# Linear attention on one core: transposes in two halves, and one store in three pieces

## The chip, the cores and the metric

The kernel runs on 1 core of one Trainium2 chip. The metric is the device time in microseconds. A run of the kernel is compared with runs of the kernel before on the same chip. The profile is of one execution; its span goes from the first to the last instruction, and the measured time has about one microsecond around it.

## The reference

```python
# q, k, v: (1, 32, 2048, 128) bf16
phi_q = jnp.where(q > 0, q + 1, jnp.exp(q)) + 1e-6
phi_k = jnp.where(k > 0, k + 1, jnp.exp(k)) + 1e-6
kv = jnp.einsum("bhsd,bhse->bhde", phi_k, v)
z = jnp.einsum("bhsd->bhd", phi_k)
num = jnp.einsum("bhqd,bhde->bhqe", phi_q, kv)
den = jnp.einsum("bhqd,bhd->bhq", phi_q, z)[..., None] + 1e-6
return num / den
```

There are 32 heads, and each is independent of the others: a 128 x 128 matrix kv with the sum z beside it is built from k and v, and each row of q is multiplied by it and divided by its denominator.

## The kernel before

One head is 2048 rows of 128 numbers. A row block lies as 128 partitions with 16 consecutive rows each, so that a load or a store of a head is one transfer of 512 KB in which each partition holds 4 KB in one piece, in SBUF and in DRAM alike. The 16 rows of a partition are the 16 "tiles" j of the head. Loads have 7 buffers for each of q, k and v (`NI`), the output has 12 (`NO`).

The function phi is computed as min(exp(x), 1) + 1e-6 plus max(x, 0). The two parts are never added; both go through TensorE and are summed in PSUM. For each head h there are these steps, named as in the order lists:

- **ldk, ldq, ldv** (L338): the loads, issued by SP in a list written out by hand; ldv0 alone is issued by ScalarE.
- **ek** (L350, ScalarE) is exp(k); **em** (L353, VectorE) the minimum and the 1e-6 on it; **rkp** (L360, GpSimd) max(k, 0), for head 0 half of it as **rkd** (L356, VectorE); **v1** (L364, GpSimd) copies v beside a column of ones, which **v1ones** (L324, VectorE) sets once.
- **kv** (L371, TensorE): 32 matmuls, two for each tile, summed into one PSUM region; **kvs** (L376, VectorE) copies it to SBUF.
- **T** (L383, TensorE): 16 transposes of q into the PSUM tensor `xT`, of which there is one only. Its 16 tiles fill two PSUM banks, tiles 0 to 7 and 8 to 15.
- **eq** (L387, ScalarE) is exp of `xT`, **emq** (L389, VectorE) the minimum and the 1e-6 on it; **rqa** (L393, ScalarE) is max(q, 0) of tiles 0 to 7, **rqb** (L396, VectorE) of tiles 8 to 15. As `xT` is single, T of head h must wait until eq, rqa and rqb of head h-1 have read it.
- **n** (L407, L412, L414, TensorE): the numerators and denominators, in groups of tiles: n.0 has 12 tiles, n.1 has 4.
- **a** (L427), **r** (L430), **f** (L434), all VectorE: the 1e-6, the reciprocal, and the product that writes the output buffer. f of head h waits until the store of head h-12 has read its buffer.
- **st** (L442, SP): the store, in the same list as the loads; head 31's goes in three transfers.

Each engine works through a fixed list (`ORDER`), one step after the other. A step waits for the steps that it names (`add(engine, name, what, deps)`), by semaphores that count: one for each engine, and one for each DMA buffer. `resolve` drops a wait that an earlier wait of the same engine implies. In the middle of the kernel TensorE's list is n(h-2).0, T(h), n(h-2).1, kv(h), n(h-1).0, T(h+1) and so on. At the beginning it is w2 w1 T0.0 T0.1 w0 T1 kv0.0 kv0.1 n0.0 kv1 T2, where w are matmuls on the identity that write nothing of use (L329).

Before, heads 0 and 31 have their transposes in two halves (`HALVES`), each a step of its own; the 30 heads between have one step of 16 transposes, which waits for all of eq, rqa and rqb of the head before.

Of the kernel before, what the change touches and what calls it, by code (L numbers as in the profile page):

```python
# [6 lines left out]
P = 128  # L7
EPS = 1e-6
ENGINES = ("PE", "DVE", "ACT", "POOL", "SP")
NH = 32  # L10
BY_ACT = ('ldv0.0',)
NI, NO, NE, NR, NV, NQ, NK = 7, 12, 2, 2, 2, 2, 2
WARM = (2, 8, 4)
HALVES = ((0, 8), (8, 16))
WHOLE = ((0, 16),)
# [13 lines left out]
def q_parts(h):  # L29
    return HALVES if h == 0 else ((0, 8), (8, 12), (12, 16)) if h == NH - 1 else WHOLE  # L30
# [23 lines left out]
def na(h):  # L54
    return NA[h]


def groups(h):
    if h == NH - 1:
        return ((0, 2, 3, 0), (6, 2, 3, 2), (12, 2, 2, 4))  # L60
    return ((0, 4, 3, 0), (12, 2, 2, 4))


def st_parts(h):
    return ((0, 6), (6, 12), (12, 16)) if h == NH - 1 else WHOLE


def gate(name, h):
# [13 lines left out]


def t_parts(h):
    return HALVES if h in (0, NH - 1) else WHOLE


def rqb_parts(h):
    if na(h) == 16:
        return ()  # L90
    if h == NH - 1:
# [3 lines left out]

ORDER = {
    "PE": """
        w2 w1 T0.0 T0.1 w0 T1.0 kv0.0 kv0.1 n0.0 kv1.0 T2.0 n0.1 kv2.0 n1.0 n1.1 T3.0 kv3.0 n2.0 T4.0 n2.1 kv4.0
        n3.0 T5.0 n3.1 kv5.0 n4.0 T6.0 n4.1 kv6.0 n5.0 T7.0 n5.1 kv7.0 n6.0 T8.0 n6.1 kv8.0 n7.0 T9.0 n7.1 kv9.0
        n8.0 T10.0 n8.1 kv10.0 n9.0 T11.0 n9.1 kv11.0 n10.0 T12.0 n10.1 kv12.0 n11.0 T13.0 n11.1 kv13.0 n12.0  # L100
        T14.0 n12.1 kv14.0 n13.0 T15.0 n13.1 kv15.0 n14.0 T16.0 n14.1 kv16.0 n15.0 T17.0 n15.1 kv17.0 n16.0
        T18.0 n16.1 kv18.0 n17.0 T19.0 n17.1 kv19.0 n18.0 T20.0 n18.1 kv20.0 n19.0 T21.0 n19.1 kv21.0 n20.0
        T22.0 n20.1 kv22.0 n21.0 T23.0 n21.1 kv23.0 n22.0 T24.0 n22.1 kv24.0 n23.0 T25.0 n23.1 kv25.0 n24.0
        T26.0 n24.1 kv26.0 n25.0 T27.0 n25.1 kv27.0 n26.0 T28.0 n26.1 kv28.0 n27.0 T29.0 n27.1 kv29.0 n28.0
        T30.0 n28.1 kv30.0 n29.0 T31.0 T31.1 n29.1 kv31.0 n30.0 n30.1 n31.0 n31.1 n31.2
    """,
    "DVE": """
        eps0 ones emq0.0 em0.0 em0.1 rqb0.0 rkd0.0 v1ones0 v1ones1 eps1 emq0.1 em1.0 eps2 kvs0 emq1.0 r0.0
# [39 lines left out]
        ldq15.0 ldv14.0 ldv15.0 ldq16.0 ldk14.0 ldk15.0 ldk16.0 ldv16.0 ldv17.0 ldk17.0 st1.0 st2.0 ldq17.0  # L148
        ldq18.0 ldk18.0 ldv18.0 ldk19.0 ldv19.0 ldk20.0 ldq19.0 st3.0 ldv20.0 ldv21.0 st4.0 ldq20.0 ldk21.0
        ldq21.0 st5.0 ldk22.0 st6.0 ldq22.0 st7.0 st8.0 ldv22.0 ldk23.0 ldk24.0 ldv23.0 ldk25.0 ldv24.0 ldk26.0  # L150
        ldv25.0 st9.0 ldq23.0 st10.0 st11.0 st12.0 ldq24.0 ldk27.0 ldv26.0 ldk28.0 ldq25.0 ldv27.0 st13.0
        ldk29.0 ldq26.0 ldq27.0 ldk30.0 ldv28.0 st14.0 ldv29.0 st15.0 ldq28.0 ldv30.0 ldq29.0 ldk31.0 st16.0
        ldq30.0 st17.0 st18.0 st19.0 ldv31.0 st20.0 ldq31.0 st21.0 st22.0 st23.0 st24.0 st25.0 st26.0 st27.0
        st28.0 st29.0 st30.0 st31.0 st31.1 st31.2
# [13 lines left out]
class Program:  # L168
# [10 lines left out]
    def add(self, eng, key, fn, deps=(), dma=None, inc=True):  # L179
        assert key not in self.op, key  # L180
        self.op[key] = (eng, fn, tuple(deps), dma, inc)
# [71 lines left out]
def bass_standalone__linear_attn_elu__prompt_kernel(nc: bass.Bass, q: bass.AP, k: bass.AP, v: bass.AP, out: bass.AP):  # L253
# [8 lines left out]
    qf, kf, vf, of = (t.rearrange("b h s d -> (b h) s d") for t in (q, k, v, out))  # L262
    rows = lambda t, h: t[h].rearrange("(p j) d -> p j d", j=NT)

    with ExitStack() as es:
# [17 lines left out]
        o_sb = sb([P, NO, NT, D])  # L283
        ident, ones, epsr = sb([P, P]), sb([P, P]), sb([P, 3])
# [7 lines left out]
        add = pr.add  # L292

        def over(name, h, parts, t0, t1):
            return [f"{name}{h}.{i}" for i, (a, b) in enumerate(parts(h)) if a < t1 and t0 < b]

        def every(name, h, parts):
            return [f"{name}{h}.{i}" for i in range(len(parts(h)))]

        def freed(n, h, *names):  # L300
            return [d for name, parts in names for d in every(name, h - n, parts)] if h >= n else []
# [5 lines left out]
        def rqs(h, t0=0, t1=NT):  # L307
            return ([f"rqa{h}"] if t0 < na(h) else []) + over("rqb", h, rqb_parts, t0, t1)
# [32 lines left out]
        def head(h):  # L341
            for i, (a, b) in enumerate(ld_parts(h)):
                load("k", k_sb, kf, h, i, a, b, freed(NI, h, ("ek", k_parts), ("rkd", rkd_parts), ("rkp", rkp_parts)))
            for i, (a, b) in enumerate(ld_parts(h)):
                load("q", q_sb, qf, h, i, a, b, freed(NI, h, ("T", t_parts)))
# [21 lines left out]
            for i, (a, b) in enumerate(kv_parts(h)):  # L367
                def g(e, a=a, b=b):
                    for j in range(a, b):
                        for part, src in ((0, em_sb[:, h % NE]), (1, rk_sb[:, h % NR])):  # L370
                            ins = e.matmul(kv_ps, lhsT=src[:, j], rhs=v1_sb[:, h % NV, j, 0:NC],  # L371
                                           start=(j + part == 0), stop=(j == NT - 1 and part == 1))
                    return ins
# [6 lines left out]
            for i, (a, b) in enumerate(t_parts(h)):  # L380
                def g(e, a=a, b=b):
                    for j in range(a, b):
                        ins = e.transpose(xT[:, j], q_sb[:, h % NI, j], ident[:])  # L383
                    return ins
                add("PE", f"T{h}.{i}", g, over("ldq", h, ld_parts, a, b) + ["ident"] + ((every("eq", h - 1, q_parts) + rqs(h - 1)) if h else []))
            for i, (a, b) in enumerate(q_parts(h)):
                add("ACT", f"eq{h}.{i}", lambda e, a=a, b=b: e.activation(emq_sb[:, h % NQ, a:b], xT[:, a:b], ACT.Exp),  # L387
                    over("T", h, t_parts, a, b) + freed(NQ, h, ("n", groups)))
                add("DVE", f"emq{h}.{i}", lambda e, a=a, b=b: e.tensor_scalar(  # L389
                    emq_sb[:, h % NQ, a:b], emq_sb[:, h % NQ, a:b], 1.0, EPS, op0=ALU.min, op1=ALU.add), [f"eq{h}.{i}"])  # L390
# [9 lines left out]
            for i, (t0, nb, m, b0) in enumerate(groups(h)):  # L400
# [31 lines left out]
                def g(e, t0=t0, t1=t1, nb=nb, m=m, b0=b0):  # L432
# [5 lines left out]
                        in1=_ap(rden_sb[:, :, :], first(rden_sb[:, h % 2, t0:t0 + 1]) - first(rden_sb[:, :, :]),  # L438
                                [[m, nb], [1, m], [0, D]]), op=ALU.mult)
                add("DVE", f"f{h}.{i}", g, [f"r{h}.{i}"] + freed(NO, h, ("st", st_parts)))  # L440
            for i, (a, b) in enumerate(st_parts(h)):
                add("SP", f"st{h}.{i}", lambda e, a=a, b=b: e.dma_start(rows(of, h)[:, a:b], o_sb[:, h % NO, a:b]),  # L442
                    [f"f{h}.{j}" for j, (t0, nb, m, b0) in enumerate(groups(h)) if t0 < b and a < t0 + nb * m],
                    dma=f"o{h % NO}")

        for h in range(NH):
            head(h)
# [40 lines left out]
```

## Time and profile before

| what | us |
|---|---|
| median of 3 runs | 169.9 |
| lowest and highest run | 169.78, 169.95 |
| span of the profiled execution | 168.8 |
| DVE busy in it | 153.7 |
| ACT busy in it | 149.6 |
| POOL busy in it | 93.8 |
| first full store (st0) issued, last store issued | 27.2, 166.0 |

The rows of a profile have the line of the kernel, the engine, the operation, what it writes and reads (all tiles of this kernel are called `la`), shapes, and the number of instructions. In a timeline the first two numbers are start and length in us; in brackets stands the idle time of the engine before, and what ended it. PEld are the weight loads of TensorE, which overlap its matmuls. The "share" of a DMA queue is the time of its packets as a part of the time of all 16 DMA engines; in a window it can be a little over 1. A transfer has landed when all engines that carry it are done.

### The profile page before, as it was taken

The numbers are of one execution on the slowest core, as the hardware profiler recorded it, in microseconds if no ns is written. First come the engines' busy times: TensorE is split into PE (matmuls) and PEld (weight loads), VectorE is DVE, ScalarE is ACT, GpSimd is POOL, SyncE is SP. The second block draws the span as 40 slices with busy tenths as digits, with TensorE's granted clock in tenths as the row PEclk, the third lists the DMA queues.
The fourth block names the chain that finished last, engine by engine and source line by source line (L and its number), as shares of the span: only waits on it lengthen the run. The fifth ranks groups of instructions, "written<-read, shape, count | busy, mean of one in ns | idle before, by whom it ended". The sixth has DMA issues, their size and how long they took to land.

```text
span 168.8 us, 6160 instructions
## 1 busy us (share of the span) xinstructions
PE 155.6 (92%) x2702; PEld 151.2 (90%) x2702; DVE 153.7 (91%) x300; ACT 149.6 (89%) x102; POOL 93.8 (56%) x71
## 2 busy tenths in 40 slices
PE   6809999999999999999999999999999999999950
PEld 2309899999999999999999999999999999999940
DVE  0094999999999999999999999999999999999993
ACT  3694799999999999999999999999999999996800
POOL 1291895566666555555666665555555667742000
PEclk9996999999999999999999999999999999999996
DMA  5999999999999999999999999999999999999986
GB/s 200 398 417 411 413 403 408 411 405 414 412 405 413 404 412 405 406 416 412 409 413 413 418 415 419 411 414 418 414 420 410 411 418 418 418 416 414 402 323 249
DMA packets 18747, 67.51 MB, mean 400 GB/s; under 512 B 2080, under 2 KB 2464, under 8 KB 18720
## 3 DMA queue, kind: packets, MB, share of 16 engines
q1 hardware_dynamic: 18576, 66.59, 98.2%
q10 hardware_dynamic: 144, 0.52, 0.8%
q8 instruction: 21, 0.34, 0.8%
q14 instruction: 6, 0.05, 0.1%
HBM read 50.33 MB, written 16.78 MB: 398 GB/s over the span
## 4 chain that ended last, share of the span: by engine, by line
PE 85%; DVE 8%; DMA 3%; ACT 1%; issue 0%; SPq 0%
PE la L371 34%; PE la L412 18%; PE la L383 17%; PE la L414 16%; DVE la L434 4%; DMA la<-in_q_dram 3%; DVE la L389 2%; DVE la L353 1%; DVE la L430 1%; ACT la L387 1%; PE la L407 0%; DVE la L396 0%; DVE la L376 0%; SPq L338 0%; DVE la L427 0%
## 5 line engine op out<-in xcount | busy, mean ns | idle before, releaser
L434 DVE TENSOR_TENSOR la<-la 128x1536 bf16<-128x1536 f32 (+2 forms) x65 | 77.7, 1197 | 0.2
L360 POOL TENSOR_SCALAR la<-la 128x2048 bf16<-128x2048 bf16 (+1 forms) x32 | 59.8, 1869 | 29.3 <-PE la L371 23.6
L414 PE MATMUL la<-la 128*128 128x129 bf16 x512 | 67.1, 220 | 0.0
L412 PE MATMUL la<-la 128*128 128x129 bf16 x512 | 67.1, 219 | 0.0
L387 ACT ACTIVATE la<-la 128x2048 bf16<-128x2048 bf16 (+2 forms) x35 | 60.2, 1730 | 6.6 <-PE la L383 3.8
L350 ACT ACTIVATE la<-la 128x2048 bf16<-128x2048 bf16 (+1 forms) x33 | 61.3, 1860 | 3.6 <-DMA la<-in_k_dram 1.9
L371 PE MATMUL la<-la 128*128 128x129 bf16 x1024 | 64.0, 222 | 0.0
L371 PEld LDWEIGHTS la<-la 128*128 128x128 bf16 x1024 | 60.2, 99 | 0.0
L364 POOL COPY la<-la 128x1024 int32<-128x1024 int32 (+1 forms) x33 | 34.6, 1051 | 29.4 <-PE la L371 25.3
L414 PEld LDWEIGHTS la<-la 128*128 128x128 bf16 x512 | 49.6, 97 | 0.0
L412 PEld LDWEIGHTS la<-la 128*128 128x128 bf16 x512 | 47.9, 97 | 0.3 <-DVE la L434 0.2
L383 PE MATMUL la<-la 128*128 128x128 bf16 x512 | 34.7, 222 | 5.0 <-DVE la L396 4.2
L383 PEld LDWEIGHTS la<-la 128*128 128x128 bf16 x512 | 30.5, 99 | 6.1 <-ACT la L350 4.6
L393 ACT ACTIVATE la<-la 128x1024 bf16<-128x1024 bf16 (+1 forms) x32 | 33.5, 1046 | 0.0
L389 DVE TENSOR_SCALAR la<-la 128x2048 bf16<-128x2048 bf16 (+2 forms) x35 | 25.4, 729 | 7.6 <-ACT la L387 7.6
L353 DVE TENSOR_SCALAR la<-la 128x2048 bf16<-128x2048 bf16 (+1 forms) x33 | 23.9, 726 | 0.0
L407 PE MATMUL la<-la 128*128 128x3 bf16 (+1 forms) x128 | 21.6, 169 | 2.0 <-DVE la L434 1.6
L396 DVE TENSOR_SCALAR la<-la 128x1024 bf16<-128x1024 bf16 x31 | 20.5, 662 | 0.0
L407 PEld LDWEIGHTS la<-la 128*128 128x128 bf16 x128 | 12.5, 98 | 2.4 <-DVE la L434 1.8
L430 DVE RECIPROCAL la<-la 128x12 f32<-128x12 f32 (+2 forms) x65 | 12.9, 200 | 1.0
L376 DVE CAST la<-la 128x129 bf16<-128x129 f32 x32 | 7.8, 242 | 2.5 <-PE la L371 2.5
L329 PE MATMUL la<-la 128*128 128x480 bf16 x14 | 5.2, 543 | 1.5 <-POOL la L314 1.5
(16 smaller groups left out, 10.7 us busy)
## 6 DMA issues: line engine op xcount, KB each, us to landing
la<-in_k_dram SPq DMA_DIRECT2D x32, 512.0 KB, 15.3
la<-in_q_dram SPq DMA_DIRECT2D x32, 512.0 KB, 15.5
la<-in_v_dram SPq DMA_DIRECT2D x31, 512.0 KB, 15.8
out_dram<-la SPq DMA_DIRECT2D x31, 512.0 KB, 15.4
la<-in_v_dram ACTq DMA_DIRECT2D x1, 512.0 KB, 5.1
out_dram<-la SPq DMA_DIRECT2D x2, 192.0 KB, 2.7
out_dram<-la SPq DMA_DIRECT2D x1, 128.0 KB, 2.7
```

The costliest lines, as they stand in the source:

```text
L350: add("ACT", f"ek{h}.{i}", lambda e, a=a, b=b: e.activation(em_sb[:, h % NE, a:b], k_sb[:, h % NI, a:b], ACT.Exp), over("ldk", h, ld_parts ...
L360: add("POOL", f"rkp{h}.{i}", lambda e, a=a, b=b: e.tensor_scalar(rk_sb[:, h % NR, a:b], k_sb[:, h % NI, a:b], BIG, 0.0, op0=ALU.min, op1=A ...
L364: add("POOL", f"v1{h}.{i}", lambda e, a=a, b=b: e.tensor_copy(v1_sb[:, h % NV, a:b, 0:D].bitcast(i32), v_sb[:, h % NI, a:b].bitcast(i32)), ...
L371: ins = e.matmul(kv_ps, lhsT=src[:, j], rhs=v1_sb[:, h % NV, j, 0:NC], start=(j + part == 0), stop=(j == NT - 1 and part == 1))
L383: ins = e.transpose(xT[:, j], q_sb[:, h % NI, j], ident[:])
L387: add("ACT", f"eq{h}.{i}", lambda e, a=a, b=b: e.activation(emq_sb[:, h % NQ, a:b], xT[:, a:b], ACT.Exp), over("T", h, t_parts, a, b) + fr ...
L389: add("DVE", f"emq{h}.{i}", lambda e, a=a, b=b: e.tensor_scalar(emq_sb[:, h % NQ, a:b], emq_sb[:, h % NQ, a:b], 1.0, EPS, op0=ALU.min, op1 ...
L393: add("ACT", f"rqa{h}", lambda e: e.activation(rq_sb[:, h % NQ, 0:n], xT[:, 0:n], ACT.Relu), over("T", h, t_parts, 0, n) + freed(NQ, h, (" ...
L407: e.matmul(_ap(o_ps[:, :], o + D, [[NC, m]]), lhsT=ones[:], rhs=epsr[:, 0:m], start=True, stop=False, skip_group_check=True)
L412: e.matmul(to, lhsT=emq_sb[:, h % NQ, t], rhs=kvs_sb[:, h % NK, 0:NC], start=late and c == 0, stop=False, skip_group_check=True)
L414: ins = e.matmul(to, lhsT=rq_sb[:, h % NQ, t], rhs=kvs_sb[:, h % NK, 0:NC], start=False, stop=True, skip_group_check=True)
L434: return e.tensor_tensor(out=_ap(o_sb[:, :, :, :], first(o_sb[:, h % NO, t0, 0:1]) - first(o_sb[:, :, :, :]), [[m * D, nb], [D, m], [1, D] ...
```

## The change

All heads have their transposes in two steps, T(h).0 and T(h).1, next to each other in TensorE's list. Each half waits only for the readers of its own tiles: T(h).0 for eq and rqa of the head before, T(h).1 for eq and rqb. For head 1, whose predecessor has eq in halves, T1.0 waits for eq0.0 and T1.1 for eq0.1.

The store of head 12, one transfer of 128 partitions, becomes three, of partitions 0 to 50, 51 to 114 and 115 to 127. They are issued one after the other at the same place of SP's list. What waits for the store waits for all three.

```diff
+ROWS = {12: ((0, 51), (51, 115), (115, 128))}
+
 def st_parts(h):
-    return ((0, 6), (6, 12), (12, 16)) if h == NH - 1 else WHOLE
+    tiles = ((0, 6), (6, 12), (12, 16)) if h == NH - 1 else WHOLE
+    return tuple((a, b, x, y) for a, b in tiles for x, y in ROWS.get(h, ((0, P),)))
...
 def t_parts(h):
-    return HALVES if h in (0, NH - 1) else WHOLE
+    return HALVES
...
-        w2 w1 T0.0 T0.1 w0 T1.0 kv0.0 kv0.1 n0.0 kv1.0 T2.0 n0.1 kv2.0 n1.0 n1.1 T3.0 kv3.0 n2.0 T4.0 n2.1 kv4.0
+        w2 w1 T0.0 T0.1 w0 T1.0 T1.1 kv0.0 kv0.1 n0.0 kv1.0 T2.0 T2.1 n0.1 kv2.0 n1.0 n1.1 T3.0 T3.1 kv3.0 n2.0 T4.0 T4.1 n2.1 kv4.0
...
-        ldv25.0 st9.0 ldq23.0 st10.0 st11.0 st12.0 ldq24.0 ldk27.0 ldv26.0 ldk28.0 ldq25.0 ldv27.0 st13.0
+        ldv25.0 st9.0 ldq23.0 st10.0 st11.0 st12.0 st12.1 st12.2 ldq24.0 ldk27.0 ldv26.0 ldk28.0 ldq25.0 ldv27.0 st13.0
...
-                add("PE", f"T{h}.{i}", g, over("ldq", h, ld_parts, a, b) + ["ident"] + ((every("eq", h - 1, q_parts) + rqs(h - 1)) if h else []))
+                add("PE", f"T{h}.{i}", g, over("ldq", h, ld_parts, a, b) + ["ident"] + (over("eq", h - 1, q_parts, a, b) + rqs(h - 1, a, b) if h else []))
...
-            for i, (a, b) in enumerate(st_parts(h)):
-                add("SP", f"st{h}.{i}", lambda e, a=a, b=b: e.dma_start(rows(of, h)[:, a:b], o_sb[:, h % NO, a:b]),
+            for i, (a, b, x, y) in enumerate(st_parts(h)):
+                add("SP", f"st{h}.{i}", lambda e, a=a, b=b, x=x, y=y: e.dma_start(
+                    rows(of, h)[x:y, a:b], o_sb[x:y, h % NO, a:b]),
                     [f"f{h}.{j}" for j, (t0, nb, m, b0) in enumerate(groups(h)) if t0 < b and a < t0 + nb * m],
                     dma=f"o{h % NO}")
```

More of the change, by code (lines that the diff above doesn't have):

```diff
@@ L97 @@
     "PE": """
-        w2 w1 T0.0 T0.1 w0 T1.0 kv0.0 kv0.1 n0.0 kv1.0 T2.0 n0.1 kv2.0 n1.0 n1.1 T3.0 kv3.0 n2.0 T4.0 n2.1 kv4.0
[L99 to L105, printed above, removed]
+        w2 w1 T0.0 T0.1 w0 T1.0 T1.1 kv0.0 kv0.1 n0.0 kv1.0 T2.0 T2.1 n0.1 kv2.0 n1.0 n1.1 T3.0 T3.1 kv3.0 n2.0 T4.0 T4.1 n2.1 kv4.0
+        n3.0 T5.0 T5.1 n3.1 kv5.0 n4.0 T6.0 T6.1 n4.1 kv6.0 n5.0 T7.0 T7.1 n5.1 kv7.0 n6.0 T8.0 T8.1 n6.1 kv8.0 n7.0 T9.0 T9.1 n7.1 kv9.0
+        n8.0 T10.0 T10.1 n8.1 kv10.0 n9.0 T11.0 T11.1 n9.1 kv11.0 n10.0 T12.0 T12.1 n10.1 kv12.0 n11.0 T13.0 T13.1 n11.1 kv13.0 n12.0
+        T14.0 T14.1 n12.1 kv14.0 n13.0 T15.0 T15.1 n13.1 kv15.0 n14.0 T16.0 T16.1 n14.1 kv16.0 n15.0 T17.0 T17.1 n15.1 kv17.0 n16.0
+        T18.0 T18.1 n16.1 kv18.0 n17.0 T19.0 T19.1 n17.1 kv19.0 n18.0 T20.0 T20.1 n18.1 kv20.0 n19.0 T21.0 T21.1 n19.1 kv21.0 n20.0
+        T22.0 T22.1 n20.1 kv22.0 n21.0 T23.0 T23.1 n21.1 kv23.0 n22.0 T24.0 T24.1 n22.1 kv24.0 n23.0 T25.0 T25.1 n23.1 kv25.0 n24.0
+        T26.0 T26.1 n24.1 kv26.0 n25.0 T27.0 T27.1 n25.1 kv27.0 n26.0 T28.0 T28.1 n26.1 kv28.0 n27.0 T29.0 T29.1 n27.1 kv29.0 n28.0
+        T30.0 T30.1 n28.1 kv30.0 n29.0 T31.0 T31.1 n29.1 kv31.0 n30.0 n30.1 n31.0 n31.1 n31.2
     """,
```

## The prediction

> **What bounds the kernel now.** I read the page's head first, then a window over the steady part with the waits of TensorE inside it, then the beginning in order of time, and last the landings of the final stores.
>
> ```profile
> span 168.8 us, 6160 instructions
> ...
> PE 155.6 (92%) x2702; PEld 151.2 (90%) x2702; DVE 153.7 (91%) x300; ACT 149.6 (89%) x102; POOL 93.8 (56%) x71
> ...
> q1 hardware_dynamic: 18576, 66.59, 98.2%
> ...
> q8 instruction: 21, 0.34, 0.8%
> ...
> PE 85%; DVE 8%; DMA 3%; ACT 1%; issue 0%; SPq 0%
> ```
>
> The chain that ended last is 85% TensorE, but one DMA queue is busy for 98.2% of the span too. Two limits lie on top of each other, and neither may be read alone.
>
> ```profile
> 20.00:160.00 140.00, 140.00 (x2540) 139.51 (x2538) 138.93 (x273) 136.32 (x91) 84.77 (x59) 1.00 1.03 412
> ```
>
> This window's columns are length, PE, PEld, DVE, ACT, POOL, clock, DMA share, GB/s. From 20 to 160 us TensorE has no hole at all: 140.00 of 140.00 us. So no wait at a transpose can be removed there; there is none. The transposes' one long wait on VectorE is at the beginning:
>
> ```profile
> PE la L383 <- DVE la L396: 4.2, 1, 4.2
> ```
>
> The last stores show the other limit. Of each the issue and the time from issue to landing, for st28, st29, st30 and st31.2:
>
> ```profile
> L442 SPq DMA_DIRECT2D out_dram<-la x1: 333/333/333, 155.8 to 155.8; - x1
> DMA to landing us min/median/max: 9.1/9.1/9.1
> ...
> L442 SPq DMA_DIRECT2D out_dram<-la x1: 332/332/332, 159.8 to 159.8; - x1
> DMA to landing us min/median/max: 6.5/6.5/6.5
> ...
> L442 SPq DMA_DIRECT2D out_dram<-la x1: 332/332/332, 163.0 to 163.0; - x1
> DMA to landing us min/median/max: 4.4/4.4/4.4
> ...
> L442 SPq DMA_DIRECT2D out_dram<-la x1: 332/332/332, 166.0 to 166.0; - x1
> DMA to landing us min/median/max: 2.7/2.7/2.7
> ```
>
> They are issued 4.0, 3.2 and 3.0 us apart, yet the first three land at 155.8 + 9.1 = 164.9, 166.3 and 167.4: 1.25 us apart, one after the other. A landing counts when the last of the 16 DMA engines is done, so the latest engines are still working without pause here; a whole store is 128 rows, 8 packets for each engine, and 1.25 / 8 = **0.156 us a packet**. They finish with the last store at 166.0 + 2.7 = 168.7, which is the end of the span. Yet over the same stretch:
>
> ```profile
> 162.00:164.00 2.00, 2.00 (x36) 1.91 (x36) 1.90 (x5) 0.00 (x0) 0.00 (x0) 1.00 0.64 256
> ```
>
> the 16 engines are busy only 0.64 of the time: some 0.36 x 16 = 6 engines have run dry while the others still have a backlog. The queues are **uneven by several microseconds**, and the span ends with the late ones. Part of the unevenness has a name: the 21 instruction fetches of 0.34 MB / 21 = 16 KB (q8) each hold up one engine for about four packets.
>
> **Transposes in halves, steady part.** T(h) waited for its load, for eq and rqa (ScalarE) and for rqb (VectorE). After the change T(h).0 waits for load, eq and rqa, T(h).1 for rqb too. The same 16 transposes issue, and the waits are shared out, not added to. Head 31 is cut already, so the cost of a cut stands in the trace, whole head 30 above, cut head 31 below:
>
> ```profile
> 150.47 1.06 PE L383 MATMUL la<-la 128*128 128x128 bf16 x16
> ...
> 155.09 1.06 PE L383 MATMUL la<-la 128*128 128x128 bf16 x16
> ```
>
> Both 1.06. At the rows' resolution of 0.01 us, 30 more cuts cost 0.3 us at the very most; I take 0, since the waits are met before TensorE gets there. Behind T(h).1 on TensorE stand n(h-2).1 and kv(h), in the same place as before.
>
> **Transposes in halves, head 1.** Here the wait is real.
>
> ```profile
> L338 SPq DMA_DIRECT2D la<-in_q_dram x1: 463/463/463, 2.7 to 2.7; - x1
> DMA to landing us min/median/max: 8.1/8.1/8.1
> ...
> 9.44 1.03 ACT L393 ACTIVATE la<-la 128x1024 bf16<-128x1024 bf16 x1
> 11.85 0.68 DVE L396 TENSOR_SCALAR la<-la 128x1024 bf16<-128x1024 bf16 x1
> 12.45 0.94 DVE L356 TENSOR_SCALAR la<-la 128x1024 bf16<-128x1024 bf16 x1
> 12.63 1.86 PE L383 MATMUL la<-la 128*128 128x128 bf16 x16 [4.19 <-DVE la L396]
> 13.34 0.13 DVE L324 MEMSET la<- 128x32 bf16 x2
> 14.29 2.74 PE L371 MATMUL la<-la 128*128 128x129 bf16 x32
> ```
>
> The load ldq1 lands at 2.7 + 8.1 = 10.8; rqa0 (L393) ends at 10.47. So T1.0 runs at 10.8, inside the old hole, and only T1.1's 8 transposes are left at 12.63, behind rqb0 (L396). Before, 16 of them kept kv0 until 14.29, 1.66 us; 8 take 0.83, and kv0.0 could begin at 13.46. What is late next is rkd0 (L356, ends 13.39) and the memset of v1's ones (L324, ends 13.47): a tie, so about **13.5, 0.8 us earlier**. What that is worth at kv0's end depends on the clock:
>
> ```profile
> 5.60:9.06 3.46, 2.02 (x21) 1.06 (x19) 0.39 (x1) 1.95 (x3) 0.80 (x1) 1.00 1.02 417
> 9.06:12.47 3.41, 0.00 (x0) 0.00 (x0) 3.41 (x5) 3.21 (x3) 2.99 (x4) 1.00 1.03 419
> 12.47:15.88 3.41, 3.25 (x31) 3.28 (x32) 2.01 (x8) 1.35 (x1) 0.64 (x1) 0.50 1.02 408
> 15.88:19.30 3.42, 3.03 (x56) 2.85 (x54) 2.23 (x2) 2.76 (x3) 2.18 (x2) 1.00 1.03 411
> ```
>
> An idle stretch of 3.41 us is followed by 3.41 us at half clock, then full clock. If the half clock still ends at 15.88, the 8 transposes saved let 8 later matmuls run in that stretch, and the gain is 8 full-speed matmuls, 8 x 1.06 / 16 = 0.5 us. If the 0.5 us of T1.0 keep the clock up, T1.1 takes 0.5 from 12.63, kv0 still waits for 13.47, then takes half of 2.74 or a little more: it ends near 15.4 instead of 17.03, a gain of 1.6. So TensorE gets ahead by **0.5 to 1.6 us** at 17 us. [...]
>
> Little of this reaches the end. The loads come no sooner because TensorE is ahead, and late loads of q are just in time:
>
> ```profile
> L338 SPq DMA_DIRECT2D la<-in_q_dram x1: 488/488/488, 124.3 to 124.3; - x1
> DMA to landing us min/median/max: 16.8/16.8/16.8
> ...
> 141.23 1.06 PE L383 MATMUL la<-la 128*128 128x128 bf16 x16
> ...
> L338 SPq DMA_DIRECT2D la<-in_q_dram x1: 1240/1240/1240, 140.1 to 140.1; - x1
> DMA to landing us min/median/max: 14.7/14.7/14.7
> ```
>
> ldq28 lands at 141.1, T28 starts at 141.23; ldq31 lands at 154.8, T31 starts at 155.09. A head start over 0.1 to 0.3 us ends in a new wait of L383 for a q load. And the span ends with the late DMA engines at 168.7, whose work is not touched by this edit. Its own term at the end: **0**, at best 0.1 from stores in the tail.
>
> **The store of head 12.** It issues at 104.3 in a queue of some 15 us:
>
> ```profile
> L442 SPq DMA_DIRECT2D out_dram<-la x1: 434/434/434, 104.3 to 104.3; - x1
> DMA to landing us min/median/max: 15.5/15.5/15.5
> ```
>
> Two more issues of 0.43 us on SP push ldq24 and all that follow on that queue by 0.9 us at issue; with 15 us between issue and landing the engines do not notice: 0. f24, which reuses the buffer twelve heads later, waits for all three pieces instead of one; with no hole in TensorE's work between 20 and 160 us, stores are nowhere what holds f up: 0. The bytes are the same. What changes is the share of each engine, and no row shows a transfer whose rows are not a multiple of 16. Two readings bound it. If rows are spread as evenly as can be, each engine gets 7 to 9 packets instead of 8: -0.16 to +0.16 us. If every engine used gets the same number of whole rows, 51 = 3 x 17 goes to three engines with 17 packets each, 64 to sixteen with 4, 13 to thirteen with 1. Then three engines get 22 packets, 14 more than now: 14 x 0.156 = **+2.2 us** on them; ten get 5, 3 fewer: **-0.47**; three get 4: -0.62. [...]
>
> Which sign the end sees depends on whether the three loaded engines are among the six that run dry. Those have at least two microseconds to spare (0.64 over 162 to 164), so +2.2 fits into their idle time, while the late ones lose 3 packets. [...] Term: **-0.47**, ends -0.62 and +2.2.
>
> **Sum.** 168.8 + 0 - 0.47 = 168.3 us of span. The compute side allows it: the last store would now issue at 166.0 with stores this late landing in as little as 2.3 us,
>
> ```profile
> DMA to landing us min/median/max: 2.3/3.8/9.1
> ```
>
> 168.3, and it issues earlier itself, as ldq28 and ldq31 land 0.4 earlier and TensorE's head start lets it use that. The median of 169.9 is 1.1 above the profiled span; so **169.4 us**, own range 169.0 to 169.7.
>
> **Rivals.** (1) *Even shares, or the relief misses the last engine.* The DMA end stays at 168.7, the 0.5 to 1.6 us of the beginning turn into a wait for q loads: 169.8, between 169.6 and 170.1. For it: no row shows an uneven split. Against: nothing in the trace evens shares out otherwise. (2) *The three loaded engines are late ones.* Then everything behind st12 lands 2.2 us later from 120 us on: ldq28 and ldq31, with 0.1 and 0.3 us to spare, stall TensorE, and the end goes to 169.9 + 2.2 = 172.1; with engines in the middle of the field that become the last it is less, 170.2 to 171. It decides as soon as their lag before st12 plus 2.2 exceeds that of today's latest. For it: 10 of 16 are not dry at 162 us. [...] (3) *The clock sets the end.* If DMA were not the second limit, the beginning's 1.6 us would show in full: 168.3. Against: landings 1.25 us apart to the last store; I give it almost nothing.
>
> **Chances.** Forecast 0.57, rival (1) 0.2, rival (2) 0.21 (a third of it below 171), rival (3) 0.02. A measurement tells some 0.2%, 0.34 us, from no change. Of the forecast's 0.57 about 0.47 lie below 169.56 and the rest within 0.2%; adding the rivals: faster 0.50, same 0.28, slower 0.22. Range 168.9 to 171.0: it holds the forecast, rival (1) and the mild part of rival (2).
>
> **What would show it.** In the changed profile: eight transposes near 10.8 us and eight at 12.63; the clock at 0.5 or 1.0 in the window from 12.47; kv0's end at 16.5 or 15.4; short waits of L383 for in_q loads after 120 us; st12's pieces on SP with their landings; ldq28 and ldq31 landing about 0.4 us earlier; stores still 1.25 us apart, ending 0.4 earlier. Landings later by one to two microseconds from 120 us on, with TensorE waiting there, would prove the store's term wrong in sign; unchanged landings would prove shares even.

## The result, and the profile after

The changed kernel takes **169.38 us** (median of 11 runs, 169.29 to 169.78), the kernel before 169.90 us (169.78 to 170.07) on the same chip. The ratio is 0.9972, with an interval of 0.9963 to 0.9981: 0.5 us faster. A second measurement on another chip (e10 below) gave 0.9975 (0.9966 to 0.9983). Forecast were 169.4 us.

The page of the changed kernel, its head and the DMA part; lines of the code are four further down than before (L383 is now L387, L442 is L446):

```profile
span 167.9 us, 6162 instructions
...
DMA packets 18763, 67.51 MB, mean 402 GB/s; under 512 B 2096, under 2 KB 2480, under 8 KB 18736
```

The same line of the page before:

```profile
DMA packets 18747, 67.51 MB, mean 400 GB/s; under 512 B 2080, under 2 KB 2464, under 8 KB 18720
```

The bytes are equal, and there are 16 more packets, all of them under 512 B. The count of these small packets is 2080 = 130 x 16 before, for 130 transfers, and the semaphore events of the trace have 2080 landings, 16 for each transfer. Three pieces on 16 engines each would add 48 - 16 = 32. It is 16, and 3 + 16 + 13 - 16 = 16: the count fits the piece of 51 partitions on **three engines**, that of 64 on sixteen, that of 13 on thirteen. The 3 + 16 + 13 = 32 landings of the pieces stand in the semaphore events, from 115.38 to 118.84 us.

The last four stores of the changed kernel, issue and landing as in the prediction:

```profile
L446 SPq DMA_DIRECT2D out_dram<-la x1: 332/332/332, 155.4 to 155.4; - x1
DMA to landing us min/median/max: 8.6/8.6/8.6
...
L446 SPq DMA_DIRECT2D out_dram<-la x1: 333/333/333, 159.4 to 159.4; - x1
DMA to landing us min/median/max: 6.0/6.0/6.0
...
L446 SPq DMA_DIRECT2D out_dram<-la x1: 332/332/332, 162.7 to 162.7; - x1
DMA to landing us min/median/max: 3.8/3.8/3.8
...
L446 SPq DMA_DIRECT2D out_dram<-la x1: 333/333/333, 165.8 to 165.8; - x1
DMA to landing us min/median/max: 2.1/2.1/2.1
```

They still land one after the other, at 164.0, 165.4, 166.5 and 167.9, some 0.8 to 0.9 us earlier than before (164.9, 166.3, 167.4, 168.7). Half of that is not the change's. The first transposes, T0, which the change doesn't touch, wait for ldq0; before and after they start at

```profile
6.96 1.07 PE L383 MATMUL la<-la 128*128 128x128 bf16 x16 [0.82 <-DMA la<-in_q_dram]
```
```profile
6.52 0.71 PE L387 MATMUL la<-la 128*128 128x128 bf16 x5
```

In this one execution the first loads landed 0.44 us earlier, and the whole DMA queue is earlier by that from the first load on. What is left of the 0.84 at the end is about 0.4. A profile is one execution; the ratio over the runs is the measure.

Head 1 in order of time, after the change:

```profile
10.50 0.68 PE L387 MATMUL la<-la 128*128 128x128 bf16 x8 [2.05 <-ACT la L397]
11.42 0.68 DVE L400 TENSOR_SCALAR la<-la 128x1024 bf16<-128x1024 bf16 x1
12.16 1.04 PE L387 MATMUL la<-la 128*128 128x128 bf16 x8 [0.97 <-DVE la L400]
13.09 3.65 PE L375 MATMUL la<-la 128*128 128x129 bf16 x32
```

T1.0 runs in the old hole, T1.1 behind rqb0 (L400), and kv0 follows T1.1 at once. The stretches of the clock (length, PE, PEld, DVE, ACT, POOL, clock, DMA share, GB/s), then the steady part and the tail:

```profile
7.51:10.92 3.41, 1.36 (x19) 0.89 (x16) 2.27 (x3) 3.33 (x4) 3.09 (x3) 1.00 1.03 419
10.92:14.33 3.41, 2.44 (x24) 2.04 (x22) 3.16 (x9) 2.42 (x2) 1.35 (x2) 0.50 1.02 416
14.33:17.75 3.42, 3.03 (x30) 2.77 (x28) 0.97 (x2) 1.75 (x2) 0.92 (x1) 0.50 1.02 408
17.75:21.16 3.41, 3.41 (x65) 3.41 (x63) 3.23 (x6) 2.13 (x3) 2.64 (x3) 1.00 1.03 410
20.00:160.00 140.00, 139.99 (x2543) 139.72 (x2540) 138.61 (x273) 136.52 (x91) 84.68 (x59) 1.00 1.02 412
162.00:164.00 2.00, 1.84 (x35) 1.66 (x31) 1.92 (x5) 0.00 (x0) 0.00 (x0) 1.00 0.73 289
```

The clock is at half for two stretches here, 6.8 us, not for one: kv0's 32 matmuls take 3.65 us instead of 2.74, and what T1.0 had gained is lost again. TensorE's middle is as dense as before. In the tail the DMA share is 0.73 where it was 0.64 (and 0.68 with the halves alone, e1 below): fewer engines have run dry. By the landings of st27, engine by engine, six stood within 0.7 us of the earliest before, and three within 0.3 us after; the last one stands 4.8 us behind the earliest where it was 5.0.

### The profile page after: what moved, and what is told of

Same layout as the page of the kernel before. It is cut to its first block, busy times and chain, and to the rows that moved or that the text cites. A ratio compares the mean times of both kernels' runs of the same rounds, so it can differ in the third digit from the quotient of the medians.

```text
span 167.9 us, 6162 instructions
## 1 busy us (share of the span) xinstructions
PE 157.2 (94%) x2702; PEld 152.2 (91%) x2702; DVE 153.1 (91%) x300; ACT 149.5 (89%) x102; POOL 94.0 (56%) x71
## 4 chain that ended last, share of the span: by engine, by line
PE 91%; DVE 6%; ACT 1%; issue 0%; POOL 0%; POOLq 0%
PE la L375 36%; PE la L416 18%; PE la L387 17%; PE la L418 17%; PE la L333 3%; DVE la L438 3%; DVE la L357 1%; DVE la L393 1%; ACT la L391 1%; DVE la L434 1%; PE la L411 0%; DVE la L400 0%; DVE la L380 0%; POOL la L318 0%; POOL la L317 0%
## 5 line engine op out<-in xcount | busy, mean ns | idle before, releaser
L387 PE MATMUL la<-la 128*128 128x128 bf16 x512 | 34.9, 222 | 3.0 <-ACT la L397 2.1
L387 PEld LDWEIGHTS la<-la 128*128 128x128 bf16 x512 | 30.6, 99 | 4.6 <-ACT la L397 2.5
L393 DVE TENSOR_SCALAR la<-la 128x2048 bf16<-128x2048 bf16 (+2 forms) x35 | 24.7, 709 | 7.6 <-ACT la L391 7.6
L411 PE MATMUL la<-la 128*128 128x3 bf16 (+1 forms) x128 | 21.5, 168 | 2.1 <-DVE la L438 1.7
L400 DVE TENSOR_SCALAR la<-la 128x1024 bf16<-128x1024 bf16 x31 | 20.5, 662 | 0.0
L411 PEld LDWEIGHTS la<-la 128*128 128x128 bf16 x128 | 12.6, 98 | 2.5 <-DVE la L438 1.8
## 6 DMA issues: line engine op xcount, KB each, us to landing
la<-in_v_dram SPq DMA_DIRECT2D x31, 512.0 KB, 15.4
```

What stands on the lines that cost most here:

```text
L411: e.matmul(_ap(o_ps[:, :], o + D, [[NC, m]]), lhsT=ones[:], rhs=epsr[:, 0:m], start=True, stop=False, skip_group_check=True)
```

## The experiments

Two theories stood against each other: that the gain comes from the late DMA engines, which lose three packets, and that it comes from TensorE's head start. Each ratio is against the kernel before, run on the same chip beside it, with its interval. The order lists change with the edits, as steps get other names; that part of the diffs is shown for e8 alone.

**One part alone.** The halves without the store (e1), and the store without the halves (e2):

```diff
-ROWS = {12: ((0, 51), (51, 115), (115, 128))}
+ROWS = {}
```
```diff
 def t_parts(h):
-    return HALVES
+    return HALVES if h in (0, 31) else WHOLE
```

> The transposes in halves as in the change, the store of head 12 whole. Theory 'late DMA engines' (the span ends with the engines that are behind, and only the store's shares move that): 0 to 0.1 us faster than before, ratio 0.9995 to 1.000. Rival 'head start' (the 0.3 us or more that TensorE gains at head 1 runs through to the end): the whole gain of the change, ratio 0.997, 169.4 us.

> The store of head 12 in 51, 64 and 13 partitions, the transposes as before. 'Late DMA engines': the late engines lose 3 packets, 0.47 us; the last store's own issue may hold back a little of it: ratio 0.997 to 0.998, 169.4 to 169.6 us. 'Head start': no change, ratio 1.000.

Measured: e1 0.9994 (0.9985 to 1.0004), e2 0.9985 (0.9976 to 0.9995). The halves alone bring nothing that can be told from zero, so the head start is not what the gain comes from: by that theory e1 has the whole gain and e2 none. The store alone brings 0.25 us by its ratio, about half of the change's gain and less than expected. By its median it brings 0.39 us (169.77 against 170.16): the runs of e2 fall into two groups, six from 169.56 to 169.77 us and five from 169.92 to 170.19. Its interval overlaps the change's, and the two parts added up, 0.9979, lie within the change's interval too; that they bring more together than one by one is not shown. What the store may lack here is taken up again in e11.

**Only head 1 cut (e3).**

```diff
 def t_parts(h):
-    return HALVES
+    return HALVES if h in (0, 1, 31) else WHOLE
```

> Halves for heads 0, 1 and 31 alone, and the store in three. Both theories: the same time as the whole change, ratio 0.997; the other 29 cuts cost and bring nothing. If the cuts of the middle heads cost something, this one is faster than the change; if they bring something, slower.

Measured: 0.9974 (0.9963 to 0.9984), the time of the change. The 29 other cuts neither cost nor bring anything that shows.

**Three pieces that share evenly (e4).**

```diff
-ROWS = {12: ((0, 51), (51, 115), (115, 128))}
+ROWS = {12: ((0, 32), (32, 96), (96, 128))}
```

> The whole change, but the store of head 12 in pieces of 32, 64 and 32 partitions, which can be shared evenly by 16 engines (8 packets each in all). 'Late DMA engines': the three transfers alone bring nothing, the time of the halves alone, ratio 0.9995 to 1.000. Rival 'three transfers' (smaller transfers land or issue better, whatever the shares): the whole gain, ratio 0.997.

Measured: 1.0002 (0.9993 to 1.0011). The gain is gone; it is the shares, not the number of transfers. (The profiled execution of e4 also lost TensorE time behind a late load of v, as e5's below, with T31 at 156.00. What speaks for the shares without that is the landing of st28, which comes as late as with the whole store; it is taken up below, with the store's term.) The page of e4 confirms how they fell, 32 small packets more than before:

```profile
DMA packets 18779, 67.51 MB, mean 400 GB/s; under 512 B 2112, under 2 KB 2496, under 8 KB 18752
```

**The same relief behind the last load (e5).**

```diff
-ROWS = {12: ((0, 51), (51, 115), (115, 128))}
+ROWS = {24: ((0, 51), (51, 115), (115, 128))}
```

> The whole change, but it is the store of head 24 that goes in 51, 64 and 13 partitions, and head 12's is whole. This store is issued behind the last load. Theory 'only the end' (the late engines' last stores are all that counts): the same gain as the change, ratio 0.997. Theory 'loads too' (TensorE's head start is only worth something if the loads after 120 us also land earlier; else it is lost at heads 28 to 31): less gain, ratio 0.998 to 1.000, and T31 no earlier than 155.

Measured: 0.9984 (0.9973 to 0.9995), less than the change, as "loads too" had it, though the intervals overlap. The trace shows what the loads do. Transposes of heads 2, 28 and 31 in e5:

```profile
19.94 1.06 PE L387 MATMUL la<-la 128*128 128x128 bf16 x16
...
140.99 0.61 PE L387 MATMUL la<-la 128*128 128x128 bf16 x8
...
155.68 1.06 PE L387 MATMUL la<-la 128*128 128x128 bf16 x16
```

TensorE was 0.8 us ahead of the kernel before at head 2 (19.94 against 20.71) and is 0.6 us behind it at head 31 (155.68 against 155.09). Of these 1.36 us, 0.53 go ahead of T28 (140.99 against 141.23), where n (L411) waits 0.57 us for emq; then from T28 to T31 three heads took 14.69 us instead of 3 x 4.62 = 13.86. GpSimd and VectorE of e5 just ahead of that:

```profile
136.01 1.04 POOL L368 COPY la<-la 128x1024 int32<-128x1024 int32 x1 [3.35 <-DMA la<-in_v_dram]
137.02 1.89 POOL L364 TENSOR_SCALAR la<-la 128x2048 bf16<-128x2048 bf16 x1
139.01 1.34 POOL L368 COPY la<-la 128x1024 int32<-128x1024 int32 x1
```
```profile
137.78 1.68 DVE L393 TENSOR_SCALAR la<-la 128x2048 bf16<-128x2048 bf16 x1
139.38 1.52 DVE L357 TENSOR_SCALAR la<-la 128x2048 bf16<-128x2048 bf16 x1
```

The copy v1 of head 28 waits 3.35 us for ldv28; GpSimd's steps behind it come late, and beside them VectorE's emq and em take 1.68 and 1.52 us, where e8 below shows 0.68 for both. Each of the two ends 0.55 us after the end of a GpSimd step (139.46 after 138.91, 140.90 after 140.35). Much the same shows emq in the kernel before, which takes 1.02 us there (139.71 after 139.15). Why VectorE's steps are longer there no run shows by itself. rqb then ends late as well, and T28.1 waits 0.22 us for it.

**A second dose (e6).** The store of head 13 goes in the same three pieces as well as head 12's.

```diff
-ROWS = {12: ((0, 51), (51, 115), (115, 128))}
+ROWS = {12: ((0, 51), (51, 115), (115, 128)), 13: ((0, 51), (51, 115), (115, 128))}
```

> The whole change, and the store of head 13 goes in 51, 64 and 13 partitions too. If the three loaded engines had a spare of about 3 us before the change and have 0.2 us after it, a second dose makes them the last by about 2 us: loads after 128 us land up to 2 us later, TensorE waits for q, 171 to 171.6 us, ratio 1.007 to 1.010. If the loaded engines had much more to spare, or the pieces were shared evenly after all: a second gain or no change against the change, ratio 0.994 to 0.997.

Measured: 1.0004 (0.9995 to 1.0012), 170.14 us. The sign was expected, the size was not: the second dose takes the gain back, 0.5 us, not 1.5 to 2. In its waits one line is new, TensorE for a late load of q:

```profile
PE la L387 <- DMA la<-in_q_dram: 1.7, 1, 1.7
```

The semaphore events of the trace, which no view of the profile prints, give the landing of each of the 16 engines for a transfer. They show where the three loaded ones were. Engines' landings behind the earliest, in us, for ldq24 (next behind the store of head 12) and ldk30:

```
before  ldq24  0.0 0.0 0.1 | 0.5 0.6 0.7 | 1.7 2.1 2.9 3.2 3.2 3.3 3.5 3.5 3.5 3.5
change  ldq24  0.0 0.1 0.2 |             | 1.4 1.7 2.0 2.6 2.7 3.1 3.1 3.1 3.2 3.2 3.2 3.3 3.3
e6      ldk30  0.0 0.1 0.2 | 2.3 2.7 3.0 3.1 3.2 3.2 3.2 3.2 3.2 | 5.0 5.2 6.0 6.2
```

Before, three engines stand 0.5 to 0.7 behind the earliest; in the change that group is gone from there, and the loaded engines have joined the field at about 3, still ahead of the last. Which three they are, the 32 landings of the store's own pieces in the change tell, reckoned from the landings of the store ahead of it at 0.156 us a packet. They are met to 0.02 us on the mean if the loaded three are two of that group and one of the earliest three, and the third of the group is one of the engines with 4 packets. With any of the ten later engines among the three, the mean miss is 0.12 us or more. With a second dose (e6) three engines stand 2 to 3 us behind all the others, at 5.2, 6.0 and 6.2; the one at 5.0 came there with this transfer, behind an instruction fetch at 132.0 us. The spare of the loaded three was 2.8 to 3.5 us. One dose, 2.2 us on them and 0.47 off most of the others, uses it up nearly to the end.

**A look at which engines lag (e7).** The store of head 12 in 16 pieces of 1 to 15 and 8 partitions.

```diff
-ROWS = {12: ((0, 51), (51, 115), (115, 128))}
+ROWS = {12: ((0, 1), (1, 3), (3, 6), (6, 10), (10, 15), (15, 21), (21, 28), (28, 36), (36, 45), (45, 55),
+             (55, 66), (66, 78), (78, 91), (91, 105), (105, 120), (120, 128))}
```

> A look at which engines lag. The store of head 12 goes in 16 pieces of 1, 2, 3 and so on to 15 partitions, and one of 8. [...] The first engine gets 8 packets more than in a whole store, 1.2 us, the last 8 fewer; time within 0.5 us of the change.

Measured, once: 171.55 us, 2 us more than the change and 1.5 over what was expected. All pieces report to one semaphore, and 128 landings within 6 us could not be told apart by engine, so which engine lags by how much stays open, and with it why the pieces cost so much. The 8 packets more on one engine and 8 fewer on another, with which the expectation reckons, are not shown either. The count of small packets does fit pieces that go to as many engines as they have rows: it is 2192, and 1 + 2 + ... + 15 + 8 - 16 = 112 more than before.

**The late loads sooner (e8, e9), and the change beside them (e10).** From head 24 on, loads of q and v go ahead of loads of k that land long before their use, and ahead of stores. e8 has the store of the change, e9 the whole one. The part of SP's list that differs, with its lines broken anew:

```diff
-st12.2 ldq24.0 ldk27.0 ldv26.0 ldk28.0 ldq25.0 ldv27.0 st13.0 ldk29.0 ldq26.0 ldq27.0 ldk30.0 ldv28.0 st14.0
-ldv29.0 st15.0 ldq28.0 ldv30.0 ldq29.0 ldk31.0 st16.0 ldq30.0 st17.0 st18.0 st19.0 ldv31.0 st20.0 ldq31.0
+st12.2 ldq24.0 ldv26.0 ldq25.0 ldk27.0 ldv27.0 st13.0 ldq26.0 ldk28.0 ldq27.0 ldv28.0 ldk29.0 st14.0 ldv29.0
+ldq28.0 st15.0 ldk30.0 ldv30.0 ldq29.0 ldk31.0 ldq30.0 st16.0 ldv31.0 st17.0 ldq31.0 st18.0 st19.0 st20.0
```

> The whole change, and from head 24 on SP's list puts loads of q and v that land just in time ahead of loads of k that land 10 us early, and ahead of stores. Theory: what takes TensorE's head start away, and can turn it into a loss of 0.8 us at heads 28 to 31, is ldv28 and ldq28 landing late. Then T28 to T31 take 3 x 4.62 = 13.86 us whatever the head start is, T31 starts at T2's start + 134.1 or so, and the end is set by the late DMA engines alone: ratio 0.996 to 0.997. Rival 'the late engines are all': the order of the loads does not matter, ratio 0.997 as the change, T31 as there.

> As e8, but the store of head 12 goes whole. The late engines keep their 3 packets: last landing some 0.47 us later than in e8. If the store's part of the gain lies at the end, ratio 0.9985 to 0.9995. If it lies in the earlier landing of the loads, which this order gives too, the ratio is that of e8.

> The change itself beside e8 and e9 on this chip: ratio 0.9972 as before, if the chip does not matter.

Measured: e8 0.9968 (0.9955 to 0.9980), 169.54 us; e9 0.9997 (0.9987 to 1.0006), 169.97 us; e10 0.9975. In e8 GpSimd's copy of head 28 waits no more for its load, and VectorE's two steps have their usual length:

```profile
135.03 1.04 POOL L368 COPY la<-la 128x1024 int32<-128x1024 int32 x1 [1.73 <-PE la L375]
```
```profile
138.41 0.68 DVE L393 TENSOR_SCALAR la<-la 128x2048 bf16<-128x2048 bf16 x1
139.01 0.68 DVE L357 TENSOR_SCALAR la<-la 128x2048 bf16<-128x2048 bf16 x1
```

In e9 the head start comes through in full: T2 and T31 start at

```profile
20.08 1.06 PE L387 MATMUL la<-la 128*128 128x128 bf16 x16
...
154.24 1.06 PE L387 MATMUL la<-la 128*128 128x128 bf16 x16
```

0.6 and 0.85 us ahead of the kernel before, and yet e9 is no faster. Its last store, and that of e8:

```profile
L446 SPq DMA_DIRECT2D out_dram<-la x1: 333/333/333, 165.2 to 165.2; - x1
DMA to landing us min/median/max: 3.3/3.3/3.3
```
```profile
L446 SPq DMA_DIRECT2D out_dram<-la x1: 332/332/332, 165.7 to 165.7; - x1
DMA to landing us min/median/max: 2.4/2.4/2.4
```

e9 issues it 0.8 us before the kernel before did, and it lands at 168.5, 3.3 us later: it stands behind the late engines. e8 issues it later than e9 and ends at 168.1. With computing out of the way, the store's part is worth 169.97 - 169.54 = **0.43 us**, and the two intervals lie apart. e8's time cannot be told from the change's: their intervals overlap over most of their length.

**The store and the sooner loads without the halves (e11), and e8 again (e12).** Why had the store alone brought less than the change in e2, if it did? Either its relief was lost to loads that came late, or it needs the halves, so that the last store is issued sooner. e11 is the change with e8's order of loads, and with the transposes whole as before:

```diff
 def t_parts(h):
-    return HALVES
+    return HALVES if h in (0, 31) else WHOLE
```

> The store in 51, 64 and 13 partitions and the order of loads of e8, the transposes as before. It asks why the store alone (e2) brought only half, with single runs from 169.56 to 170.19. Theory 'late loads': in some runs ldv28 and ldq28 still come late and cost three heads up to 0.8 us; with the loads sooner the store alone brings nearly all, ratio 0.9970 to 0.9978, and the runs lie within 0.3 us. Theory 'the last store's issue': without the halves' head start the last store is issued no earlier than before, and the ratio stays at 0.998 to 0.999.

> e8 once more beside it, halves, store and loads sooner: ratio 0.9968 as measured; the difference to e11 is what the halves are worth when no load is late: 0 to 0.2 us.

Measured: e11 0.9973 (0.9962 to 0.9983), 169.60 us; e12 0.9968 (0.9956 to 0.9980), 169.50 us. Without the halves, the store and the sooner loads bring 0.45 us, nearly all; the sooner loads are worth nothing that can be told by themselves (e8 against the change, e9 against e1). So if e2 lacked something, it was the loads. That is not shown: the intervals of e2 and e11 overlap (0.9976 to 0.9995 and 0.9962 to 0.9983), and by the medians, 0.39 and 0.45 us, there is next to nothing to explain. The halves then add 0.1 us, which is not told from zero. But the eight runs of e11 lie from 169.23 to 169.93 us, not within the 0.3 us that was expected, while the five of e12 lie from 169.43 to 169.67 and the eleven of e10, the change itself, from 169.41 to 170.02. The profiled execution of e11 is its slowest, 169.93, and shows where that one lost its time. TensorE at the beginning, in order of time, and the last three stores:

```profile
12.30 1.87 PE L387 MATMUL la<-la 128*128 128x128 bf16 x16 [4.21 <-DVE la L400]
13.96 3.67 PE L375 MATMUL la<-la 128*128 128x129 bf16 x32
19.52 1.98 PE L375 MATMUL la<-la 128*128 128x129 bf16 x32
21.33 0.28 PE L387 MATMUL la<-la 128*128 128x128 bf16 x2
```
```profile
L446 SPq DMA_DIRECT2D out_dram<-la x3: 332/332/333, 164.7 to 166.6; - x3
DMA to landing us min/median/max: 1.9/2.1/2.9
```

kv0 takes 3.67 us, at half clock nearly to its end, as in the change (3.65); T2 starts at 21.33, where the change has 20.68, and TensorE keeps that lag: its last store is issued at 166.6 and lands 1.9 us later, at 168.5. No store in these profiles lands sooner than 1.9 us behind its issue, so in this one execution the issue sets the end and not the late engines. With the same poor half clock the halves start T2 0.65 us earlier; 0.1 of that is the loads', as T0 starts at 6.62 here and at 6.52 there.

## Why the prediction was right, and where its steps were not

The gain came from the store and had the size that was forecast. That the forecast was met to 0.02 us is luck: the runs of the changed kernel span 0.5 us, and when it was measured again (e10) it gained 0.4 us.

**Two limits, and the late engines set the end: right.** The last stores of the change land 1.1 to 1.4 us apart, one after the other as before, and e9, where TensorE and the last store's issue are 0.6 to 0.85 us ahead, gains nothing. Where TensorE is late it is the other limit: in the profiled executions of e4, e5 and e11, T31 starts 0.5 to 0.9 us later than in the kernel before, and the last store lands 1.9 us behind its issue, as soon as any here.

**The instruction fetches as part of the unevenness: borne out by the landings, at about twice the size.** Just ahead of the first of the 21 fetches, at 21.0 us of the kernel before, the engines land within 0.5 us of each other. Behind the 1st, the 9th and the 17th (21.0, 76.6 and 132.7 us) the largest lag goes from 0.5 to 1.7, from 2.0 to 3.3 and from 3.5 to 4.8 us, and behind most of those between them one more engine falls back towards the last ones. That is 1.15 to 1.3 us a fetch, seven or eight packets, where the prediction had four. The 21 packets of q8 themselves took 0.93 to 1.11 us each, 1.03 on the mean (0.8% of the time of 16 engines over 168.8 us). The changed kernel shows the same steps. No run moved a fetch, so the cause is read from the times alone.

**The cut itself costs nothing: right** (e3 against the change, 0.9974 and 0.9972).

**T1.0 in the old hole: right** in place (10.50, and kv0 at 13.09; forecast 10.8 and 13.5, with loads that landed 0.44 us later). **The head start of 0.5 to 1.6 us: wrong at its upper end.** That end assumed T1.0 would keep the clock up. (Its sum has a slip as well: 15.4 stands for a kv0 of 1.9 us, about what kv1 takes at full clock, 1.98, and not for half of 2.74.) The half clock came all the same: in the profiles of the change, e1, e3, e8, e9, e10 and e12 kv0 takes 3.03 (e9) to 3.65 us, where kv1 takes 1.98 at full clock. In e5 the stretches are these:

```profile
8.64:12.06 3.42, 0.61 (x8) 0.46 (x8) 3.42 (x4) 3.30 (x3) 3.02 (x4) 1.00 1.02 417
12.06:15.47 3.41, 3.14 (x29) 3.02 (x30) 2.15 (x8) 1.88 (x1) 0.79 (x1) 0.50 1.03 413
```

The stretch with 0.61 us of matmuls was followed by half clock all the same, and so was the one with 1.36 us in the change. The half clock starts at 12.06 us here, at 10.92 in the change and at 12.47 in the kernel before, and in the profiles with the cut T2 starts anywhere from 19.94 (e5) over 20.08 (e9) and 20.68 (the change) to 21.04 (e3):

```profile
21.04 0.67 PE L387 MATMUL la<-la 128*128 128x128 bf16 x9
```

The change's own profile has no head start at all at T2, 20.68 against 20.71, though its loads came 0.44 us earlier. Like for like, half clock to kv0's end in both, the cut is worth 0.5 to 0.65 us at T2 (the change against e11), the lower end of the forecast. That T1.0 would keep the clock up was the author's assumption, and no run shows it.

**A head start ends in a wait of L387 for a q load: the place was wrong, the outcome half right.** It is ldv28 first: its late copy on GpSimd comes beside VectorE's steps, and 1.36 us are lost by T31 (e5), more than the head start. The wait of L387 for a q load showed, after 20 us, only in e6 and e7. e8 and e9 remove this by the order of the loads alone and keep the 4.62 us a head. That VectorE's steps are longer because GpSimd's run beside them is the reading of the two timelines; no run measured it by itself.

**Two more issues on SP, 0.9 us for what follows: right in effect, wrong in size.** In e2, where the store of head 12 is issued 0.1 us sooner than in the kernel before, ldq24 is issued 1.9 us later (106.64 against 104.75). It lands sooner all the same, at 120.5 instead of 121.0, so nothing waits for it.

**The store of 51 rows on three engines: right**, by the 16 extra small packets and by the 32 landings of the pieces, which this split meets to 0.02 us on the mean. The second reading was an assumption before the change ran. In e4 and e7 the counts fit it too, 32 and 112 more than before.

**The three loaded engines have time to spare: right, and the choice of engines was a bet that came off.** The prediction took them for some of the six that run dry at the end and asked for 2.2 us of spare. They were three of the six early ones, at most 0.7 us behind the earliest and 2.8 or more ahead of the last. That some engines are left alone by the fetches agrees with the landings: six stay within 0.7 us of the earliest to st27. That the three are among those six no row had shown, and three engines picked blindly would be among them once in 28 times (20 of 560). At ldq24 the change leaves them just short of being last; one more dose (e6), and rival (2) happens in its mild form.

**-0.47 for the store and 0 for the halves: right, perhaps with a condition that was missed.** No row had shown which reading holds or on which engines the packets fall, and no run shows the -0.47 by itself, as 3 packets less on the late engines; what the runs show in its place is when st28 lands, and the time. Every profile shows the store's part. Counted from the landing of ldq0, st28 lands at 157.99 to 158.12 us where every store of a whole head goes whole or in even pieces (before, e1, e4, e9), and at 157.44 to 157.81 in the eight profiles with one uneven store: 0.4 us sooner on the mean. With two such stores (e6) it is 158.34, with the stairs (e7) 159.34. In time, the store measured -0.45 us in e11 and -0.43 between e9 and e8, wherever the late loads had been moved out of the way; the halves measured -0.1 (e1) and -0.1 (e12 against e11), neither told from zero. With the order of loads as it was, the store alone measured -0.25 by the ratio and -0.39 by the medians (e2). The prediction had seen ldq28 and ldq31 with 0.1 and 0.3 us to spare, and used them only to cap the halves' gain; that the store's gain could run into late loads too was not in the sum. e2's profiled execution, 169.56 us, has the full relief all the same, with its last store issued when the kernel before issued it and landed 0.5 us sooner:

```profile
L446 SPq DMA_DIRECT2D out_dram<-la x2: 332/332/332, 165.4 to 166.0; - x2
DMA to landing us min/median/max: 2.2/2.2/2.2
```

Five of the eleven runs of e2 took 169.92 to 170.19 us, and they have no profile. That they lost it to late loads rests on e11 alone, whose interval overlaps that of e2; that some were instead late at the beginning, as e11's profiled execution was, is as possible. How much each has in the scatter **stays open**. The second would give the halves a use that the median hardly shows, keeping the worst case of the clock from the end; but e10 has the halves and scatters as widely.

## What to carry to other kernels

Where a kernel's transfer engines are all busy, ask which of them is the last, not how busy they are on the mean. Here a store cut into 51, 64 and 13 rows moved packets from late engines to early ones and brought 0.43 us (e9 against e8), and it did so only as long as the early ones had time to spare: with a second store cut so (e6) the gain was gone. Where two limits lie on top of each other, look at the loads that are only just in time before measuring an edit alone: they can turn a head start into a loss (e5), and they may hide part of an edit's worth (0.25 against 0.46 us here by the ratios, whose intervals overlap). Issuing them ahead of loads that land long before their use cost nothing here. And a median beside the ratio shows whether a small gain is one or a mixture of two.

## What was not expected of the hardware

Beside GpSimd's late steps VectorE's were longer: tensor_scalar steps of 0.68 us took 1.68 and 1.52 us (e5), 1.66 and 1.52 in e4. And the clock was more often at half than thought. Behind a stretch of 3.41 us at half clock with 2.44 us of matmuls came a second one at half (10.92 to 14.33 us in the changed kernel), behind one with 3.14 us came full clock (12.06 to 15.47, e5). Behind stretches at full clock with 0.61 (8.64 to 12.06, e5) and 1.36 us of matmuls (7.51 to 10.92 in the changed kernel) came half clock, behind one with 2.02 us full clock (5.60 to 9.06 before).
